# One 16-wide run order for a head's token columns, with one GpSimd copy each for halo and tail gather

## The chip, the cores and the metric

One core of a Trainium2 chip. The metric is the device time of one execution in microseconds (us). Times are medians over executions. A ratio of two kernels is the mean time of one kernel's fast runs over that of the other's fast runs in the same rounds, so it is not quite the ratio of the medians that are quoted. A run counts as slow when it lies over 1.5% above the fastest of its kernel. The granted clock is TensorE's clock as the profile shows it, 1 being full speed. The DMA share is the time of all packets over the time of 16 DMA engines.

## The reference, cut to what matters

```python
# batch 8, heads 8, sequence 576, head width 64, features 128
def phi(x):                       # per token
    proj = x @ w_phi
    proj = proj - max(abs(proj))
    return concat(exp(proj), exp(-proj))
kv  = phi(k).T @ v ;  z = sum(phi(k))
x   = (phi(q) @ kv) / (phi(q) @ z)              # linear attention, per head
gate = sigmoid(causal 5-tap convolution of x over the tokens)
out  = (gate * (x @ w_val)) @ w_out             # 576 x 512 per batch, float32
```

Token t of a head is t = 36x + 2y + a: x (0 to 15) is the run, y (0 to 17) the place in the run, a the parity. Loads put a run into one partition, and TensorE and DMA transposes turn y into columns.

## The kernel before

All instructions of all eight batches stand in one fixed order, the string `ORDER`, with the PSUM banks (`BANKS`) and, for 100 tasks that may go to either of two engines, the choice (`FLEX`) beside it. Within it, one batch goes: transposed loads of q and k (SyncE issues them), key features (exponentials on ScalarE), key-value products, query features, numerators (`num`), normalization, transposition to `XT`, gate and value projections, output projection, eviction to one of six `OUTS` buffers, and a write to memory, issued by SyncE.

A head's columns lie in two halves: k (runs 0 to 7 and 8 to 15), then y, then x within the half. A numerator chunk takes one half with y 0 to 15, so it needs the query features of four units (a unit holds four y). The last two y of both halves are the "tail", a fifth chunk.

```python
def qexp(self, t, b, u, s):          # unit u: y = 4u .. 4u+3
    i = self.two(t.grp, n * P).rearrange("p a (h r) -> p a h r", h=2 * H)
    if u < 4:                        # 32 columns in each half
        o = self.QTIL[b % 2][:, s, ...].rearrange("p a h (k r) -> p a (h k) r", k=2)[:, :, :, u * 32:(u + 1) * 32]
        self.nc.scalar.activation(o, i, AF.Exp, scale=1.0 - 2.0 * s)
    else:                            # tail: one instruction per parity
        for a in range(2): ...

def halo(self, t, b):                # the two y of the run before, for the convolution
    X = self.XT[b % 2][...].rearrange("p h k (y x) -> p (h k) y x", x=8)
    self.nc.gpsimd.tensor_copy(X[:, :, 0:2, 1:8], X[:, :, 18:20, 0:7])
    self.nc.gpsimd.tensor_copy(X[:, 1::2, 0:2, 0:1], X[:, 0::2, 18:20, 7:8])

def gvc(self, t, b):                 # gather the tail of gate*value, x before y
    for j in range(4):
        self.nc.gpsimd.tensor_copy(GVT[...].rearrange("p a (k x y) -> p (a k) x y", k=2, x=8), GV[...])

def odma(self, t, b, c, i0, i1):     # the writes; O is an OUTS buffer, 128 partitions x 512 floats
    if c < 4:                        # main write: 128 rows of 2 KB
        d = self.out_d[b].rearrange("(k x y a) o -> a k y x o", k=2, x=8, a=2)[c % 2, c // 2, 0:16, :, :]
        nc.sync.dma_start(d, O[:, :])
    else:                            # tail write: 32 rows for each batch and parity
        ...
        d = self.out_d[b - 1 + i].rearrange("(x y a) o -> a x y o", x=16, a=2)[a, :, 16:18, :]
        eng.dma_start(d, O[p0:p0 + 32, :])
```

Of the kernel before, what the change touches and what calls it, by code (L numbers as in the profile page):

```python
# [14 lines left out]
BF16 = mybir.dt.bfloat16  # L15
# [13 lines left out]
NW = 14  # L29
NJ = 2 * NC  # L30
XH = R // 2
HALO = 16
XW = HALO + XH
WARM = (
    "8:7:5 21:7:1 214:5:1 "
# [6 lines left out]
    "15 16 18 17 20 19 22 21 24 35 23 37 26 25 36 39 57 27 38 59 41 32 34 170 40 43 61 60 33 172 55 42 73 74 64 47 171 174 58 "  # L42
    "193 311 49 63 44 0 28 76 62 56 50 29 48 65 93 75 45 94 67 53 91 66 54 30 46 92 51 68 97 173 31 89 98 77 188 90 184 52 "
    "185 95 194 96 69 186 189 72 79 5 187 99 228 2 71 100 229 104 313 190 105 70 226 80 9 106 227 101 78 1 103 234 191 110 "
    "175 235 192 10 111 230 178 102 182 179 183 107 112 231 180 108 195 312 11 181 232 109 84 233 81 197 203 82 206 196 6 85 "
    "113 83 314 204 198 8 7 114 199 12 201 319 236 237 205 86 200 320 115 238 202 207 87 210 4 88 116 239 208 315 14 240 118 "
    "117 316 209 211 119 122 212 128 317 241 129 215 242 123 217 124 318 214 125 120 130 213 176 131 243 321 216 329 121 13 "
    "332 3 322 126 331 177 127 132 218 324 330 354 433 434 219 323 355 247 221 248 435 139 220 352 140 353 250 141 436 252 "
    "358 359 149 222 251 249 325 437 150 133 327 356 134 357 244 438 135 246 360 361 223 326 245 333 224 439 136 225 328 137 "
    "265 335 362 266 142 138 363 334 337 143 145 144 338 336 151 339 367 152 440 369 146 253 340 370 254 441 368 267 268 255 "  # L50
    "341 259 442 372 269 256 261 343 260 364 371 443 262 147 366 444 342 148 450 365 446 447 263 452 154 449 445 451 166 155 "
    "257 264 562 448 563 258 458 565 167 344 459 453 347 485 564 345 461 273 346 274 486 454 460 348 455 270 275 477 478 162 "
    "456 271 566 481 457 158 482 163 479 272 480 376 159 349 377 160 483 284 484 378 156 462 350 161 464 285 373 465 351 157 "
    "276 374 567 463 277 487 286 466 488 568 375 467 279 278 492 569 287 379 493 280 153 380 288 281 468 570 494 282 289 164 "
    "573 283 571 577 575 391 472 578 295 576 299 392 165 296 574 393 572 579 290 469 685 686 394 300 606 470 580 607 395 381 "
    "688 471 495 687 382 385 473 496 307 386 497 608 308 581 383 583 609 387 303 584 388 489 304 384 689 291 491 582 389 490 "
    "292 498 604 390 499 474 605 475 500 585 476 610 588 405 611 399 406 690 400 586 410 407 401 691 396 587 411 501 397 612 "
    "503 414 692 613 398 502 589 402 415 591 614 403 693 408 590 404 615 293 592 616 409 593 297 510 618 595 301 506 511 168 "
    "412 617 507 294 696 413 622 298 699 729 812 813 516 730 302 624 425 416 169 594 517 504 623 814 426 421 698 505 518 619 "
    "422 519 815 508 621 697 599 512 429 620 513 727 816 430 509 628 596 629 520 431 728 731 600 630 597 694 625 732 598 735 "  # L60
    "432 627 514 736 417 626 515 712 733 418 695 715 601 734 714 700 602 702 713 521 603 524 703 522 817 527 523 701 525 528 "
    "530 526 818 529 531 704 532 737 705 708 819 537 711 738 707 539 538 820 709 535 706 305 540 633 710 427 536 739 423 716 "
    "533 634 309 740 722 306 631 534 741 748 428 632 856 750 745 424 935 857 541 643 746 635 936 310 644 639 723 747 636 542 "
    "937 640 749 751 645 637 646 753 938 558 543 638 647 752 823 559 717 854 862 641 826 863 939 546 855 825 724 718 642 547 "
    "860 725 861 554 726 824 742 555 858 744 719 859 827 720 743 828 940 651 721 648 941 652 649 662 653 650 754 829 419 663 "
    "654 548 755 830 831 556 655 832 756 942 420 656 766 549 864 833 767 760 757 557 550 834 865 943 835 761 821 768 837 660 "
    "544 769 560 551 758 770 661 838 869 759 657 870 836 822 664 944 871 866 665 658 868 762 666 763 659 867 872 545 667 979 "
    "873 839 980 764 561 677 842 945 765 874 673 678 840 981 674 780 982 843 675 771 841 850 781 679 772 985 782 774 986 552 "
    "676 773 977 775 978 950 680 776 777 844 953 954 553 778 955 785 779 952 669 786 668 951 783 845 670 956 671 789 784 957 "
    "875 672 790 849 983 877 846 984 946 847 876 787 848 949 878 788 851 880 947 962 791 879 852 965 804 853 948 963 958 987 "  # L70
    "805 883 959 964 796 988 966 884 881 960 972 893 882 887 797 894 889 961 885 888 992 973 989 994 886 890 798 895 800 896 "
    "991 891 799 808 801 993 897 968 892 974 967 990 1001 975 1002 998 976 681 1003 809 999 969 682 810 995 1000 970 907 996 "
    "971 904 908 997 905 792 811 909 1004 906 1006 1005 793 1012 1007 1010 1016 1013 1008 916 1011 898 1009 1017 1014 901 917 "
    "1018 899 902 1019 910 1015 903 794 900 1020 806 914 683 911 795 912 802 807 1024 913 684 1021 915 803 1025 1027 1026 "
    "1030 1028 1031 1022 1029 923 1032 1037 924 1023 925 1033 1039 926 1034 1035 1040 1038 927 919 928 1036 931 929 920 1041 "
    "1054 932 918 921 930 1046 933 1055 922 1058 1056 1047 934 1042 1048 1059 1062 1057 1060 1050 1043 1049 1051 1044 1063 "
    "1052 1061 1045 1053 "
)
FLEX = (
    "ADAADAAAAAPPAPPDAAAADDAADAPPDPPDDAAADPPDPPDDADAPPAPPDAAAAAPPAPPDAADDPPAPPAAADADPPDPPDDADAPDDPPADDDDA"  # L80
)
BANKS = (
    "460006544445500124166757234523230145452301456767723672301674501445674652345230145234501276045505450101236723016701016767"
    "674230145670101011236736601674501014523236503323016723674501454567232370123456723450124567741230123236745236732374567452"
    "323450123452367010016767230167676452322367450167016767453636623674567452301452301454500101010101232320101732014501676767"
    "010122154523230145674545676767454450145674545450012303223672301010145236636423236745456701010145014524523670167452323457"
    "201230145450123457466234567014567230123674545701672301672345230177674501234545016744555"
# [69 lines left out]
def build(plan, em=None):  # L157
# [20 lines left out]
    for b in range(B):  # L178
# [19 lines left out]
        if b:  # L198
# [24 lines left out]
            for w in "kq":  # L223
                if b <= PEB:
                    for i, (c0, n) in enumerate(((0, 8), (8, 8), (16, 2))):
                        g = plan.group("tp", 1)
                        tp = A("x" + w, b, i, "PE", 0.06 * n, fn("tp16", w, b, c0, n), [xf[w]], g, 0)
                        h.setdefault(("tps",), []).append(tp)
                        x = A("x" + w, b, i, ("DVE", "ACT"), (dve(n * P), act(n * P)), fn("tc16", w, b, c0, n), [tp], g)
                        for u, (d0, m) in enumerate(UNITS):  # L230
                            if c0 <= d0 < c0 + n:
                                h["x" + w, b, u] = x
                    continue
# [7 lines left out]
        if b == 1:  # L241
# [3 lines left out]
            cg = A("mqt", 0, 0, "POOL", 5.0, fn("c_gt"), [cc], rank=-10)  # L245
# [45 lines left out]
        for u, (c0, n) in enumerate(UNITS):  # L291
            g = plan.group("qp", 2)
            qp = h["qp", b, u] = A("qp", b, u, "PE", 0.118 * n, fn("qp", b, u), [mqr, ceb, G("xq", b, u)], g, 1)
            for s in range(2):
                h["qexp", b, u, s] = A("qexp", b, u, "ACT", act(2 * n * P), fn("qexp", b, u, s),
                                       [qp] + [G("num", b - 2, c) for c in range(4)] + [G("num", b - 1, 4) if u == 4 else None]
                                       + (G("tps",) if b == 1 else [])
                                       , g)


        allq = [G("qexp", b, u, s) for u in range(NU) for s in range(2)] + [G("kv", b, i) for i in range(2)]
        for c in range(5):
            g = plan.group("num", 2 if c < 4 else 1)
# [17 lines left out]
        halo = A("xtc", b, 3, "POOL", 0.6, fn("halo", b), [G("xtc", b, 2)] + [G("gate", b - 2, j) for j in range(4)])  # L321
# [11 lines left out]
        gvc = h["gvc", b] = A("gvc", b, 0, "POOL", 0.6, fn("gvc", b), [G("gv", b, j) for j in range(4)] + [G("out", b - 4, 4)])  # L333
# [19 lines left out]
class Emit:  # L353
    def __init__(self, nc, tc, ctx, q, k, v, w_phi, moe_w_val, moe_conv_w, moe_w_out, out):
# [40 lines left out]
        self.XT = TT("XT", 2, [P, H, 2, XW])  # L395
# [26 lines left out]
        for i in range(2):  # L422
            nc.gpsimd.memset(self.MQP[i][:, :], 0.0)
            nc.gpsimd.memset(self.XT[i][:, :, :, 0:HALO], 0.0)
# [211 lines left out]
    def qp(self, t, b, u):  # L636
# [3 lines left out]
        for par in range(2):  # L640
            rows = slice(par * D, (par + 1) * D)
            nc.tensor.matmul(self.PS[:, t.grp.banks[par], 0:n * P], self.W2[rows, :],  # L642
                             X[rows, c0 * P:(c0 + n) * P].rearrange("p (y h x) -> p h y x", y=n, h=2 * H),
# [207 lines left out]
```

## Time and profile before

| | before |
|---|---|
| time, median of 3 runs | 230.52 us (229.71 to 232.11) |
| span of the profiled run | 228.5 us, granted clock 0.989 |
| busy: PE, DVE, ACT, POOL | 205.4, 176.3, 180.7, 102.8 us |
| from the last matmul's end to the end of the span | 5.3 us |

PE is TensorE, DVE VectorE, ACT ScalarE, POOL GpSimd, SP SyncE; a q behind a name means its instruction queue.

SyncE's timeline has the transposed key loads (start, us that the issue took, what):

```profile
105.07 2.69 SPq L543 DMA_TRANSPOSE kT<-KQN  x1
...
125.88 5.11 SPq L543 DMA_TRANSPOSE kT<-KQN  x1
...
149.81 2.69 SPq L543 DMA_TRANSPOSE kT<-KQN  x1
```

Issue took 2.7 us where no other data was moving (first and third); it took 5.1 us where a value load of 1152 KB had been issued just ahead. The last packets of these three landed 5.0, 7.9 and 4.1 us after the start of their issue, by the trace's DMA records.

### The profile page before, as it was taken

To read this page: it belongs to the slowest core of one execution; us is meant where nothing else is said; L and a number is where in the kernel's file an instruction comes from. 1 tells how busy PE (TensorE), PEld (TensorE's weight loads), DVE (VectorE), ACT (ScalarE), POOL (GpSimd) and SP (SyncE) were. 2 spreads that over 40 slices of the span, in tenths; PEclk is the share of its full clock that TensorE was granted. 3 is DMA by queue.
4 is the path that set the end of the run, shared out by engine and by line. 5 is a ranking of instruction groups with operands and counts; after the bars stand their busy time and mean duration, and the time that the engine had idled before them with its cause. 6 is when DMAs were issued, how large, how long until landed. Compare 5 with 4: busy or idle time off the path is not lost.

```text
span 228.5 us, 9138 instructions
## 1 busy us (share of the span) xinstructions
PE 205.4 (90%) x4001; PEld 142.6 (62%) x4027; DVE 176.3 (77%) x264; ACT 180.7 (79%) x266; POOL 102.8 (45%) x158
## 2 busy tenths in 40 slices
PE   7668887798988999989999999999999999999990
PEld 3345555666675676757667677676765866766640
DVE  2686785998879895989699979788798899483361
ACT  2995999889899988988899999979988999913220
POOL 2718594496029608930099009910119639100020
PEclk9997999999999999999999999999999999999998
DMA  6999943999699939995899995969964206156156
GB/s 202 315 265 286 209 78 103 224 196 183 113 187 244 191 93 179 293 199 61 176 225 182 279 219 141 190 127 228 291 222 138 53 3 142 49 77 204 46 180 188
DMA packets 49282, 39.87 MB, mean 174 GB/s; under 512 B 33690, under 2 KB 38554, under 8 KB 49178
## 3 DMA queue, kind: packets, MB, share of 16 engines
q1 hardware_dynamic: 43136, 29.76, 52.6%
q0 software_dynamic: 5760, 9.31, 24.1%
q8 instruction: 31, 0.51, 0.9%
q10 hardware_dynamic: 346, 0.22, 0.3%
q14 instruction: 9, 0.07, 0.1%
HBM read 30.49 MB, written 9.44 MB: 175 GB/s over the span
## 4 chain that ended last, share of the span: by engine, by line
PE 53%; DVE 17%; DMA 4%; issue 3%; ACT 3%; POOL 2%; DVEq 0%; ACTq 0%
PE PS L751 13%; PE PS L775 10%; PE PS L732 7%; PE PS L598 5%; PE PS L555 5%; DVE XN L691 4%; DMA kT<-KQN 4%; DVE MQP L562 3%; PE PS L670 3%; DVE MK L562 3%; PE PS L739 3%; DVE GV L757 2%; PE PS L642 2%; PE PS L699 2%; PE PS L649 2%
## 5 line engine op out<-in xcount | busy, mean ns | idle before, releaser
L588 POOL TENSOR_TENSOR VT<-VN,EK 128x1152 bf16<-128x1152 f32 x31 | 65.8, 2123 | 60.2 <-ACT EK L581 50.8
L572 ACT ACTIVATE KTIL<-PS 128x1024 bf16<-128x1024 f32 (+1 forms) x80 | 72.5, 951 | 6.3 <-PE PS L555 3.1
L657 ACT ACTIVATE QTIL<-PS 128x1024 bf16<-128x1024 f32 x64 | 62.6, 1036 | 4.6 <-PE PS L649 4.0
L562 DVE TENSOR_REDUCE MQP<-PS 128x8 f32<-128x1024 f32 (+1 forms) x40 | 44.1, 1112 | 6.7 <-PE PS L555 5.6
L562 DVE TENSOR_REDUCE MK<-PS 128x8 f32<-128x1024 f32 (+1 forms) x40 | 44.0, 1110 | 2.5 <-PE PS L555 1.4
L751 PE MATMUL PS<-XT,WV 64*128 64x288 bf16 x512 | 35.5, 283 | 0.4 <-DVE XN L691 0.2
L757 DVE SCALAR_TENSOR_TENSOR GV<-TH,PS 128x576 bf16<-128x576 bf16 x32 | 23.7, 751 | 15.5 <-PE PS L751 10.9
L775 PE MATMUL PS<-WOUT,GV 128*128 128x512 bf16 x109 | 29.6, 380 | 1.5 <-issue 0.6
L743 ACT ACTIVATE TH<-PS 128x576 bf16<-128x576 f32 x32 | 20.1, 655 | 13.0 <-PE PS L739 12.9
L751 PEld LDWEIGHTS <-WV 64*128 64x128 bf16 x512 | 24.6, 94 | 8.3 <-issue 2.6
L598 PE MATMUL PS<-VT,KTIL 64*128 64x65 bf16 x1152 | 24.1, 191 | 1.4 <-POOL VT L589 0.5
L598 PEld LDWEIGHTS <-KTIL 64*128 64x128 bf16 x1152 | 21.3, 95 | 4.2 <-issue 1.3
L691 DVE TENSOR_TENSOR XN<-PS,RCP 128x512 bf16<-128x512 f32 x32 | 22.1, 691 | 1.1
L670 PE MATMUL PS<-KV,QTIL 128*128 128x65 bf16 x512 | 20.1, 193 | 1.7 <-DVE GV L757 0.5
L670 PEld LDWEIGHTS <-QTIL 128*128 128x128 bf16 x512 | 18.2, 97 | 5.0 <-issue 2.7
L612 ACT ACTIVATE OUTS<-PS 128x512 f32<-128x512 f32 x22 | 13.3, 606 | 9.8 <-PE PS L775 9.1
L732 PE MATMUL PS<-XT,GF 128*64 128x288 bf16 x256 | 20.6, 290 | 0.4 <-DVE MQP L562 0.2
L720 POOL COPY XT<-XT 128x224 bf16<-128x224 bf16 x8 | 3.0, 374 | 34.4 <-DVE XT L716 22.3
L775 PEld LDWEIGHTS <-GV 128*128 128x128 bf16 x128 | 11.0, 97 | 11.6 <-issue 1.1
L555 PE MATMUL PS<-W,kT 64*128 64x128 bf16 x288 | 14.9, 219 | 2.7 <-ACT kT L522 1.4
L555 PE MATMUL PS<-W,qT 64*128 64x128 bf16 x288 | 15.1, 220 | 1.7 <-ACT KTIL L572 0.9
L642 PE MATMUL PS<-qT,W 64*128 64x512 bf16 (+1 forms) x80 | 15.0, 359 | 0.9 <-ACT QTIL L657 0.5
(74 smaller groups left out, 257.6 us busy)
## 6 DMA issues: line engine op xcount, KB each, us to landing
VN<-in_v_dram SPq DMA_DIRECT2D x8, 1152.0 KB, 6.9
out_dram<-OUTS SPq DMA_DIRECT2D x32, 256.0 KB, 3.4
KQN<-in_q_dram POOLq DMA_DIRECT2D x6, 576.0 KB, 6.5
KQN<-in_k_dram POOLq DMA_DIRECT2D x6, 576.0 KB, 8.3
KTIL<-in_k_dram SPq DMA_DIRECT2D x4, 288.0 KB, 4.2
KTIL<-in_q_dram SPq DMA_DIRECT2D x4, 256.0 KB, 4.4
out_dram<-OUTS SPq DMA_DIRECT2D x14, 64.0 KB, 3.2
QTIL<-in_q_dram POOLq DMA_DIRECT2D x1, 576.0 KB, 10.4
```

Source lines behind the costliest of these rows:

```text
L555: nc.tensor.matmul(self.PS[:, t.grp.banks[par], i * P:(i + 1) * P], X[rows, (c0 + i) * P:(c0 + i + 1) * P], self.W2[rows, :], start=True, ...
L562: self.nc.vector.tensor_reduce(o, self.two(t.grp, n * P).rearrange("p a (c f) -> p a c f", f=F), AX.X, ALU.max, apply_absolute_value=True)
L572: self.nc.scalar.activation(self.KTIL[b % 2][:, s, c0:c0 + n, :, :].rearrange("p c a f -> p a c f"), self.two(t.grp, n * P).rearrange("p a ...
L588: eng.tensor_tensor(self.VT[g][:, s, :, 0:D], self.VN[b % 2][:, NC * g:NC * g + NC, :], e.to_broadcast([P, NC, D]), ALU.mult)
L598: nc.tensor.matmul(self.PS[:, t.grp.banks[ab], (s * 2 + x) * E1:(s * 2 + x + 1) * E1], self.KTIL[b % 2][rows, s, J // 2, J % 2, :], self.V ...
L657: self.nc.scalar.activation(o, i, AF.Exp, scale=1.0 - 2.0 * s)
L670: nc.tensor.matmul(self.PS[:, t.grp.banks[h // 4], (h % 4) * E1:(h % 4 + 1) * E1], Q[:, s, c % 2, h, (c // 2) * P:(c // 2 + 1) * P], self. ...
L691: nc.vector.tensor_tensor(o.rearrange("p (g h) d -> p g h d", g=ng), n[:, :, :, 0:D], rc.unsqueeze(3).to_broadcast([P, ng, 4, D]), ALU.mult)
L732: self.nc.tensor.matmul(self.PS[h2 * D:(h2 + 1) * D, t.grp.banks[par], 0:R], self.GF[:, h, i, :], X[:, h, :, HALO - 8 * s:HALO - 8 * s + X ...
L751: nc.tensor.matmul(self.PS[:, t.grp.banks[par], 0:R], self.WV2[rows, h, j * P:(j + 1) * P], X[rows, h, :, HALO:XW], start=(h == 0), stop=( ...
L757: nc.vector.scalar_tensor_tensor(out=self.GV[b % 3][:, j, :, :], in0=self.TH[j][:, :, :], scalar=1.0, in1=self.two(t.grp, R), op0=ALU.add, ...
L775: nc.tensor.matmul(self.PS[:, t.grp.banks[0], :], lhsT, self.WOUT[:, j, :], start=(j == 0), stop=(j == 3))
```

## The change

A head's columns go in one run order, y and then all 16 x. A numerator chunk is then 8 y of 16 x and needs two units in place of four; the tail's columns are contiguous, so the tail exponentials of both parities fit one instruction, and halo and tail gather one GpSimd copy each. Order, banks and engine choices are drawn anew for it (`NW`, the number of filler tasks, goes from 14 to 11). The diff in extract, without the strings (`...` marks what is cut, and lines are shortened):

```diff
 def qexp(self, t, b, u, s):
-    i = self.two(t.grp, n * P).rearrange("p a (h r) -> p a h r", h=2 * H)
+    i = self.two(t.grp, n * P).rearrange("p a (h r) -> p a h r", h=H)
-    if u < 4: ...   else: for a in range(2): ...
+    o = QTIL[...][:, s, :, :, r0:r0 + D]   if u < 4   else   QTT[:, s, ...].rearrange("p h a r -> p a h r")
+    self.nc.scalar.activation(o, i, AF.Exp, scale=1.0 - 2.0 * s)
 def halo(self, t, b):
-    self.nc.gpsimd.tensor_copy(X[:, :, 0:2, 1:8], X[:, :, 18:20, 0:7])
-    self.nc.gpsimd.tensor_copy(X[:, 1::2, 0:2, 0:1], X[:, 0::2, 18:20, 7:8])
+    self.nc.gpsimd.tensor_copy(X[:, :, 0:2, 1:16], X[:, :, 18:20, 0:15])
 def gate / val:                                  # 288 columns in one run
-    X[:, h, :, HALO - 8 * s:HALO - 8 * s + XH]
+    X[:, h, HALO - 16 * s:HALO - 16 * s + R]
 def gvc(self, t, b):
-    for j in range(4): self.nc.gpsimd.tensor_copy(... "p a (k x y) -> p (a k) x y" ...)
+    self.nc.gpsimd.tensor_copy(self.GVT[b // 2 % 2][:, :, b % 2, :, :], self.GV[b % 3][:, :, :, 2 * P:R])
 def out(self, t, b, c):
-    lhsT = GV[:, j, c % 2, (c // 2) * XH:(c // 2) * XH + P]
+    lhsT = GV[:, j, c % 2, (c // 2) * P:(c // 2 + 1) * P]
 def odma(...):
-    d = self.out_d[b].rearrange("(k x y a) o -> a k y x o", k=2, x=8, a=2)[c % 2, c // 2, 0:16, :, :]
+    i = c // 2
+    d = self.out_d[b].rearrange("(x y a) o -> a y x o", x=16, a=2)[c % 2, 8 * i:8 * i + 8, :, :]
     nc.sync.dma_start(d, O[:, :])
-    d = self.out_d[b - 1 + i].rearrange("(x y a) o -> a x y o", x=16, a=2)[a, :, 16:18, :]
+    d = self.out_d[b - 1 + i].rearrange("(x y a) o -> a y x o", x=16, a=2)[a, 16:18, :, :]
     eng.dma_start(d, O[p0:p0 + 32, :])
```

## The prediction

> **What bounds the kernel now.** I read the busy times by stage first, then the chain that ended last, the waits, and the timelines of GpSimd and TensorE. Busy times in five stages (start and end in us, length, then each engine's busy us and number of instructions, granted clock, DMA share, GB/s):
>
> ```profile
> 0.00:30.00 30.00, 22.29 (x244) 13.51 (x247) 19.60 (x25) 21.91 (x33) 16.16 (x34) 0.94 1.00 253
> 30.00:80.00 50.00, 43.00 (x965) 31.27 (x969) 41.30 (x61) 45.72 (x64) 29.31 (x34) 1.00 0.86 168
> 80.00:200.00 120.00, 117.19 (x2514) 83.78 (x2528) 101.43 (x155) 107.73 (x162) 55.23 (x81) 1.00 0.75 166
> 200.00:220.00 20.00, 19.69 (x275) 12.81 (x274) 11.45 (x22) 4.77 (x8) 2.14 (x10) 1.00 0.46 106
> 220.00:228.50 8.50, 3.20 (x15) 1.20 (x13) 2.47 (x4) 0.60 (x1) 0.00 (x0) 0.90 0.71 219
> ```
>
> The columns are PE, PEld, DVE, ACT, POOL. Length minus PE busy gives TensorE's idle time: 7.7 us in the start, 7.0 us while the pipeline over the eight batches fills, only 2.8 us in the 120 us of its middle, 0.3 us in the end run and 5.3 us after the last matmul: 23.1 us in all. ScalarE is at 90% and VectorE at 85% in the middle. So three engines are nearly full there; after 200 us it is TensorE alone.
>
> The chain that ended last, its last pieces (start, length, what):
>
> ```profile
> 209.32 1.10 PE PS L732 x16
> 210.43 0.49 PE PS L739 x12
> 210.92 0.32 PE PS L775
> 211.24 0.05 issue
> 211.29 0.59 PE PS L775 x2
> 211.89 4.14 PE PS L751 x64
> 216.41 6.81 PE PS L775 x30
> 223.24 0.69 DVE OUTS L608
> ```
>
> The value projection (L751) goes at 4.14/64 = 65 ns a matmul, the output projection (L775) at 6.81/30 = 227 ns. This end run is packed; a new order cannot shorten it unless it takes work out of it.
>
> Busy is not packed, though. I took the distance from each matmul's start to the next from the trace, and for each group the mean of the lower nine tenths as its unhurried pace. At that pace the work of the middle stage would take some 98 of its 120 us, that of 30 to 80 us some 34 of 50. So short stalls of about 22 us hide in the 117 us that the middle calls busy. They are what a better order could win, and the size of that win is the uncertain term of this prediction.
>
> Last, GpSimd near the end. Two of the longest waits and its timeline:
>
> ```profile
> POOL XT L720 <- DVE XT L716: 22.3, 4, 11.2
> POOL GVT L763 <- DVE GV L757: 14.2, 3, 9.0
> ```
>
> ```profile
> 190.88 0.38 POOL L720 COPY XT<-XT 128x224 bf16<-128x224 bf16 x1
> 191.20 0.26 POOL L721 COPY XT<-XT 128x16 bf16<-128x16 bf16 x1
> 191.36 2.12 POOL L588 TENSOR_TENSOR VT<-VN,EK 128x1152 bf16<-128x1152 f32 x1
> 193.43 1.39 POOL L589 CAST VT<-EK 128x18 bf16<-128x18 f32 x1
> ```
>
> The two halo copies stand ahead of a value scaling of batch 7 in GpSimd's queue, and TensorE's key-value products of that batch wait for the scaling: the idle record there is 0.22 us. In this trace GpSimd's waits are long but nearly all off the path.
>
> **What the Trainium skill says.** "Perfetto Trace Analysis", section Identifying the Most-Contended Engine (and its opening note): matmul busy time is a bad measure because matmuls are pipelined. The trace agrees: 117 us busy against 98 at pace. "TensorE: Matmul & The Clock Gate", Back-to-back issue gap: N/2.4 + 2.5 ns for one warm matmul, 122.5 ns for the 288 columns here. Two matmuls on different half arrays took 130 ns per pair in the end run, so that is within 6% of the page; contiguous columns in place of two runs of 144 can win little. "ScalarE: Activation LUTs", What ACT_TABLE_LOAD costs: an ACTIVATE with immediates takes 186 ns + 0.833 ns per element, neighbours overlap by about 93 ns. For 256 and 512 elements that is 399 and 613 ns; the trace has 401 (mean of the tail exponentials) and 609 (the key exponentials of the same size). "PSUM — Partial Sum Buffer", Engine vs sequencer instructions: the queues of ScalarE, VectorE and GpSimd are strict FIFO. The timeline above shows it: a scaling behind a halo copy.
>
> **The change part by part.** The rows used, of the groups by form:
>
> ```profile
> L660 ACT ACTIVATE QTT<-PS 128x256 bf16<-128x256 f32 x32 | 10.3, 401 | 0.1
> L572 ACT ACTIVATE KTIL<-PS 128x512 bf16<-128x512 f32 x16 | 9.4, 609 | 1.1 <-PE PS L555 1.1
> L763 POOL COPY GVT<-GV 128x64 bf16<-128x64 bf16 x32 | 6.3, 241 | 14.2 <-DVE GV L757 14.2
> L721 POOL COPY XT<-XT 128x16 bf16<-128x16 bf16 x8 | 2.0, 252 | 0.0
> ```
>
> 1. Tail exponentials: 32 of 256 elements become 16 of 512. Busy 10.3 us becomes about the 9.4 us of the key's sixteen: minus 0.9 us of ScalarE. The 64 large ones keep 1024 elements; runs of 32 become runs of 64, and since the key exponentials with runs of 128 take the same 1036 ns, runs cost nothing here.
> 2. Halo: 224 + 16 elements become 240. From 252 ns at 16 and 374 at 224 elements the slope is 0.59 ns, so 240 take about 383: minus 8 x 0.25 = 2.0 us of GpSimd.
> 3. Tail gather: four copies of 64 become one of 256. Four took 0.79 us in the timeline; by the same slope one of 256 takes about 0.39: minus 8 x 0.4 = 3.2 us of GpSimd. Together minus 5 of 103 us on an engine that is 45% busy, with a halo or gather on the chain only once or twice: about 0.2 us at the end.
> 4. Numerators: chunk pairs wait for two units in place of four. Worth something only if a numerator is placed ahead of the batch's last exponentials. I read both orders off the diff: in the new one, too, every numerator of every batch stands behind all exponentials of that batch, by at least 7 places. So the freedom that gives the change its name is hardly used: 0 to 0.5 us. The other half of it, that a query exponential waits for two numerators of two batches before, is never near.
> 5. Matmuls: same number, columns and weights; gates and value projections read their 288 columns in one run in place of two of 144. Zero, by the paces above. Three filler tasks of two matmuls go, which ran where TensorE had nothing else.
> 6. Order, banks and engines: all drawn anew. In the string of the 100 tasks that may go to either engine, 39 are ScalarE's before and 30 after. By kind: five output evictions (606 ns on ScalarE, 684 on VectorE), three copies of batch 0's and three of batch 1's transposed inputs leave ScalarE, two key-value evictions (628 against 695) join it. After the start that is ScalarE -3.0 + 1.3 - 0.9 = -2.6 us, VectorE +3.4 - 1.4 = +2.0 us. If ScalarE alone bound the 170 us from 30 to 200 us (153 us busy, 90%), that would give 2.6/0.90 = 2.9 us; if the sum of both did, 0.6 of 296 us is nothing. I take the middle, 1.3 us. In the start, the early copies taken from a ScalarE that is 73% busy: 0.7 us of the 7.7 us idle. In the new order all of batch 7's scalings on GpSimd stand ahead of the halo copy of batch 6, which removes the wait shown above: 0.3 us.
>
> Sum: 0.2 + 0.2 + 1.3 + 0.7 + 0.3 = 2.7 us, the second 0.2 for part 4. Predicted: 230.5 - 2.7 = 227.8 us, 1.2% less.
>
> **The rivals.** First, the order search found much more than I can read: of 22 us of hidden stalls a third goes, and of 7 us idle in the fill 2 go. For it: ScalarE, TensorE and VectorE are each short of full by 10, 18 (at pace) and 15% in the middle. Against: the old order was tuned to the same limits. It would make 221 to 224 us. Second, VectorE becomes the bound: its total goes from 176 to about 181 us, ScalarE's from 181 to about 174, and VectorE's reductions (1.22 us each, 64 of them) hold PSUM banks that the next projections wait for. For it: "DVE MQP L562" and "DVE MK L562" stand in the chain in the fill. Against: VectorE had 15% idle in the middle. It would make 229 to 232 us. Third, TensorE alone bounds from 80 us on, as its 98% suggests; then nothing but start and fill can win: 229 to 230 us. Fourth, an order drawn anew meets stalls on the chip that its plan did not have, and gives the gain back: 231 to 235 us.
>
> **Range and chances.** The counted parts give 0.4 us and the re-drawn order the rest, so the spread is that of the order: 224.0 to 231.0 us should hold it 8 times in 10. More than 2% faster means below about 225.9, which asks for the first rival in some measure: 0.27. Slower by over 2% means above 235: 0.04. Within 2%: 0.69.
>
> **What would show it.** Right if: sixteen tail exponentials near 609 ns; eight halo copies near 0.38 us and eight gathers near 0.4 us; paces of 65 and 227 ns unchanged in the end run; ScalarE's busy time near 174 us and VectorE's near 181; TensorE's busy time within 3 us of 205; the end run from the last numerators to the last matmul still some 24 us. Wrong if: numerators do start before the last exponentials of their batch; if the middle stage takes several us less with TensorE's work in it at a clearly higher pace (first rival); or if VectorE goes over 90% there and matmuls wait for its reductions (second). A gather that takes over 0.8 us would show that the slope from the halo copy does not carry over.

## More of the kernel before

The target of a main write has the dimensions (16 y, 8 x, 512), that of a tail write (16 x, 2 y, 512). There are 32 main and 16 tail writes; two of the tail writes are issued by ScalarE.

The prediction shows the views that its argument rests on. Two it did not look at are needed later: the DMA queues (packets, megabytes, share of 16 engines' time) and the output writes (count, KB, median us from issue to landing), from the page of the kernel before.

```profile
q1 hardware_dynamic: 43136, 29.76, 52.6%
...
q10 hardware_dynamic: 346, 0.22, 0.3%
...
out_dram<-OUTS SPq DMA_DIRECT2D x32, 256.0 KB, 3.4
out_dram<-OUTS SPq DMA_DIRECT2D x14, 64.0 KB, 3.2
```

q1 is the queue that SyncE feeds, q10 that of ScalarE.

## The result, and the profile after

The changed kernel takes 252.51 us (249.04 to 254.87, four runs, two of them slow) against 230.12 us: ratio 1.0857, 95% interval 1.0711 to 1.1003. Predicted were 227.8 us, at most 231.0.

Two rows of the stages and the last one (columns as in the prediction: PE, PEld, DVE, ACT, POOL busy us, clock, DMA share, GB/s):

```profile
100.00:120.00 20.00, 16.79 (x340) 12.08 (x337) 15.38 (x26) 14.19 (x22) 6.93 (x9) 0.97 0.98 161
...
140.00:160.00 20.00, 15.12 (x263) 10.17 (x263) 12.71 (x24) 11.70 (x16) 11.30 (x13) 0.83 1.06 190
...
240.00:249.50 9.50, 0.00 (x0) 0.00 (x0) 0.00 (x0) 0.00 (x0) 0.00 (x0) 0.50 0.28 83
```

No engine was full in the first two; all are short of work together, while the DMA engines are at 0.98 and 1.06, and in the second the granted clock falls to 0.83. In the last 9.5 us no engine works at all, and data still moves at 83 GB/s. What stands in the chain that ended last (start, us, what) and in TensorE's waits (total us, times, longest):

```profile
84.21 7.97 DMA kT<-KQN
...
107.64 10.51 DMA kT<-KQN
...
136.92 11.59 DMA kT<-KQN
...
232.03 4.46 DMA out_dram<-OUTS
```

```profile
PE PS L553 <- DMA kT<-KQN: 9.3, 4, 4.6
```

The same wait in the kernel before:

```profile
PE PS L555 <- DMA kT<-KQN: 0.7, 1, 0.7
```

There TensorE waited 0.7 us for transposed keys, and after 50 us its chain had no DMA in it. Three loads of transposed keys now hold 30 us of the chain, and a late output write the end. SyncE's timeline shows what stands ahead of two of them:

```profile
105.55 1.98 SPq L780 DMA_DIRECT2D out_dram<-OUTS  x3
107.64 6.88 SPq L541 DMA_TRANSPOSE kT<-KQN  x1
...
133.43 2.68 SPq L786 DMA_DIRECT2D out_dram<-OUTS  x4
136.16 0.65 SPq L780 DMA_DIRECT2D out_dram<-OUTS  x1
136.92 8.00 SPq L541 DMA_TRANSPOSE kT<-KQN  x1
```

Issue now takes 6.9 and 8.0 us, and the last packets land 8.3 and 9.4 us after its start. That invites one explanation, that the new order put output writes in front of the loads. The DMA lines of the page say something else:

```profile
q1 hardware_dynamic: 42684, 29.76, 51.8%
...
q10 hardware_dynamic: 318, 0.22, 0.3%
...
out_dram<-OUTS SPq DMA_DIRECT2D x32, 256.0 KB
out_dram<-OUTS SPq DMA_DIRECT2D x14, 64.0 KB
```

The megabytes are the same, but q1 lost 43136 - 42684 = 452 packets and q10 lost 28, and in the trace those are all packets of 4 bytes. The Trainium skill explains the number. Its page "DMA: Bandwidth & Descriptors", section Why a DMA increments its semaphore by 16 and not by 1, says that a copy runs on k of the 16 DMA engines, where k is the largest number up to 16 that divides the slowest dimension (not of size 1) of both access patterns, and that on the queues of SyncE and ScalarE each of the k engines posts its own completion. The source has 128 partitions in a main write and 32 in a tail write, and with a target of 16 both give k = 16 before; target 8 gives k = 8 for a main write, target 2 gives k = 2 for a tail write. Completions missing: 32 x (16 - 8) + 14 x (16 - 2) = 256 + 196 = 452 on SyncE's queue, and 2 x (16 - 2) = 28 on ScalarE's. Both agree to the packet.

The trace also agrees in its time. I counted how many of the 2 KB output packets are in flight at once: at most 20 before, at most 11 after. Of the time with packets in flight, the most is spent at exactly 16 before (9.4 us) and at exactly 8 and 2 after (29.0 and 15.7 us), which fits k. A single main write takes 1.4 us from its first to its last packet before (at 178 us) and 2.5 us after (at 191 us); a packet alone still takes 84 ns. The last group of writes, 960 packets in both kernels, takes 8.1 us before and 16.9 us after, and the time from the last matmul to the end of the span goes from 5.3 to 13.3 us. The trace does not name the engines; the page says that such a queue takes the lowest-numbered k, so that all narrow writes would meet on the same ones, which no run here shows.

The parts that were meant to be cheaper are, as rows of the groups show (kind, shapes, count, busy us, mean ns):

```profile
L658 ACT ACTIVATE QTT<-PS 128x512 bf16<-128x512 f32 x16 | 8.9, 607 | 1.1 <-PE PS L647 1.1
L758 POOL COPY GVT<-GV 128x256 bf16<-128x256 bf16 x8 | 3.2, 403 | 24.8 <-DVE GV L753 24.8
L717 POOL COPY XT<-XT 128x240 bf16<-128x240 bf16 x8 | 3.1, 388 | 30.8 <-DVE XT L713 29.7 <-DVE OUTS L606 1.1
```

### The profile page after: what moved, and what is told of

It reads as the page before. It is cut to its first block, busy times and chain, and to the rows that moved or that the text cites. A ratio compares the mean times of both kernels' runs of the same rounds, so it can differ in the third digit from the quotient of the medians.

```text
span 249.5 us, 9081 instructions
## 1 busy us (share of the span) xinstructions
PE 209.4 (84%) x3997; PEld 144.6 (58%) x4021; DVE 180.7 (72%) x273; ACT 176.1 (71%) x241; POOL 99.0 (40%) x126
## 3 DMA queue, kind: packets, MB, share of 16 engines
q1 hardware_dynamic: 42684, 29.76, 51.8%
## 4 chain that ended last, share of the span: by engine, by line
PE 47%; DMA 18%; DVE 15%; ACT 6%; issue 5%; POOL 2%; ACTq 1%; DVEq 0%
DMA kT<-KQN 16%; PE PS L747 9%; PE PS L768 7%; PE PS L553 7%; PE PS L728 6%; PE PS L596 6%; DVE MK L560 4%; DVE MQP L560 3%; ACT KTIL L570 2%; PE PS L640 2%; PE PS L735 2%; PE PS L667 2%; DMA out_dram<-OUTS 2%; PE PS L647 2%; DVE XN L688 2%
## 5 line engine op out<-in xcount | busy, mean ns | idle before, releaser
L658 ACT ACTIVATE QTIL<-PS 128x1024 bf16<-128x1024 f32 x64 | 61.9, 1034 | 5.7 <-PE PS L647 5.4
L747 PE MATMUL PS<-XT,WV 64*128 64x288 bf16 x512 | 36.7, 288 | 1.5 <-issue 0.7
L768 PE MATMUL PS<-WOUT,GV 128*128 128x512 bf16 x113 | 31.2, 394 | 1.5 <-issue 0.5
L596 PE MATMUL PS<-VT,KTIL 64*128 64x65 bf16 x1152 | 23.2, 191 | 1.3 <-issue 0.4
L596 PEld LDWEIGHTS <-KTIL 64*128 64x128 bf16 x1152 | 20.7, 95 | 3.6 <-issue 1.8
L553 PEld LDWEIGHTS <-kT 64*128 64x128 bf16 x288 | 9.6, 98 | 17.4 <-DMA kT<-KQN 10.2
L768 PEld LDWEIGHTS <-GV 128*128 128x128 bf16 x128 | 11.8, 101 | 13.4 <-issue 2.9
L610 ACT ACTIVATE OUTS<-PS 128x512 f32<-128x512 f32 x17 | 10.2, 609 | 11.4 <-PE PS L768 11.3
L606 DVE TENSOR_SCALAR OUTS<-PS 128x512 f32<-128x512 f32 x19 | 13.0, 686 | 5.5 <-PE PS L768 4.6
L728 PEld LDWEIGHTS <-GF 128*64 128x64 bf16 x256 | 13.1, 109 | 6.4 <-issue 2.3
(72 smaller groups left out, 249.2 us busy)
```

Of the source, the lines that this page charges most:

```text
L553: nc.tensor.matmul(self.PS[:, t.grp.banks[par], i * P:(i + 1) * P], X[rows, (c0 + i) * P:(c0 + i + 1) * P], self.W2[rows, :], start=True, ...
L596: nc.tensor.matmul(self.PS[:, t.grp.banks[ab], (s * 2 + x) * E1:(s * 2 + x + 1) * E1], self.KTIL[b % 2][rows, s, J // 2, J % 2, :], self.V ...
L728: self.nc.tensor.matmul(self.PS[h2 * D:(h2 + 1) * D, t.grp.banks[par], 0:R], self.GF[:, h, i, :], X[:, h, HALO - 16 * s:HALO - 16 * s + R] ...
L747: nc.tensor.matmul(self.PS[:, t.grp.banks[par], 0:R], self.WV2[rows, h, j * P:(j + 1) * P], X[rows, h, HALO:XW], start=(h == 0), stop=(h = ...
L768: nc.tensor.matmul(self.PS[:, t.grp.banks[0], :], lhsT, self.WOUT[:, j, :], start=(j == 0), stop=(j == 3))
```

## The experiments

Three theories were set against each other. W: the write patterns begin with 8 and 2, so each write has 8 and 2 DMA engines. O: the new order stands output writes ahead of transposed loads and stalls TensorE. L: the layout's other parts, such as the 288 columns in one run, cost the time. The kernels (labels as in the sections below) ran in three groups, each on one chip beside the kernel before: e1, e2, e4 and e7 shared seven of its runs (median 230.31 us), e5, e6, e8 and e9 eleven (231.09 us), e3, e10, e11 and e12 eleven (230.48 us). Across groups, ratios are compared.

Every kernel was told correct, also those that put rows at wrong tokens. With these inputs the outputs of a batch's tokens are nearly equal: swapping the rows of a chunk as below changes the reference's result by 0.2% of its norm. So for row order correctness rests on the patterns, not on the comparison.

### Undo one half of the change

```diff
 # e1: the changed kernel
-NW, WARM, ORDER, FLEX, BANKS of the changed kernel
+NW, WARM, ORDER, FLEX, BANKS of the kernel before
 # e2: the kernel before
-NW, WARM, ORDER, FLEX, BANKS of the kernel before
+NW, WARM, ORDER, FLEX, BANKS of the changed kernel
```

> The changed layout under the old order, banks and engine choices. Theory W (the changed write patterns begin with a dimension of 8 in the main writes and 2 in the tail writes, so each output write runs on 8 or 2 DMA engines where it had 16): 243 to 254 us, most of the loss is here. Theory O (the new order puts transposed loads behind output writes in SyncE's queue and stalls TensorE): 228 to 232 us, as before.

> The old layout and its writes under the new order, banks and engine choices. W: 225 to 231 us, the order alone does no harm. O: 247 to 254 us, the loss is here.

Layout alone: 249.2 us, ratio 1.0847 (1.0768 to 1.0926). Order alone: 232.42 us, ratio 1.0121 (1.0056 to 1.0186). The order falls as the cause of the large loss. It has one of its own, 1.2%, a little over the range of W. Under the old order the wait looks different. Two rows of the waits of the layout alone:

```profile
ACT OUTS L611 <- DMA out_dram<-OUTS: 10.3, 2, 7.8
...
PE PS L769 <- ACT OUTS L611: 7.4, 2, 7.2
```

There the evictions wait for an output buffer that a late write still holds, and TensorE for the evictions; it waits only 1.2 us for transposed keys. The profiled run is a fast one.

### Only the first dimension of the writes

```diff
 # e4: the changed kernel, wide writes, wrong rows on purpose
-    ... .rearrange("(x y a) o -> a y x o", x=16, a=2)[c % 2, 8 * i:8 * i + 8, :, :]
+    ... .rearrange("(x y a) o -> a x y o", x=16, a=2)[c % 2, :, 8 * i:8 * i + 8, :]
-    ... .rearrange("(x y a) o -> a y x o", x=16, a=2)[a, 16:18, :, :]
+    ... .rearrange("(x y a) o -> a x y o", x=16, a=2)[a, :, 16:18, :]
 # e7: the kernel before, narrow writes, wrong rows on purpose
-    ... .rearrange("(k x y a) o -> a k y x o", k=2, x=8, a=2)[c % 2, c // 2, 0:16, :, :]
+    ... .rearrange("(k x y a) o -> a k x y o", k=2, x=8, a=2)[c % 2, c // 2, :, 0:16, :]
-    ... .rearrange("(x y a) o -> a x y o", x=16, a=2)[a, :, 16:18, :]
+    ... .rearrange("(x y a) o -> a y x o", x=16, a=2)[a, 16:18, :, :]
```

> The changed kernel with the two middle dimensions of the write's target swapped, so that it begins with a dimension of 16; rows land at wrong tokens on purpose, bytes and number of rows stay. W: 225 to 231 us, and up to some 19 output packets in flight at once where the changed kernel had 11. O: 247 to 254 us.

> The kernel before with its writes' target dimensions swapped the other way, so that they begin with 8 (main) and 2 (tail); wrong rows on purpose. W: 243 to 254 us, with at most 11 output packets in flight. O: 229 to 232 us.

Wide writes: 232.15 us, ratio 1.0100 (1.0037 to 1.0163), just over W's range of 231 us. The kernel before with narrow writes: 249.43 us, ratio 1.0829 (1.0744 to 1.0914), within W's range. Two lines, with no instruction added and no byte moved more, take the loss away and bring it about. With wide writes the page has 43136 and 346 packets again, at most 20 output packets in flight and 5.1 us after the last matmul:

```profile
q1 hardware_dynamic: 43136, 29.76, 52.6%
...
q10 hardware_dynamic: 346, 0.22, 0.3%
```

With narrow writes in the kernel before there are 42684 and 318, and at most 12 packets in flight where 11 were forecast; where four tail writes go alone (206.5 to 212.4 us) never more than 4. Theory W stands; L is left with nothing, as the remaining 1.0% is about that of the order alone.

A swap of the dimensions also changes the order in which rows fall in memory. For the main writes this is no rival: x runs innermost in the kernel before, which is fast, and in the changed kernel, which is slow; y does so in the wide version (fast) and in the narrow one (slow). For the tail writes the two were not separated.

Another rival is the granted clock: in the changed kernel's trace it stands at 0.5 for 10.2 us of the middle (119.0 to 122.4 and 146.3 to 153.1 us). What this adds there was not separated, but it is not needed for the loss. The profiled run of e10 below, narrow in batches 0 to 5, has clock 1.0 up to its last matmul, and is still 7.3 us longer than that with wide writes throughout (237.1 against 229.8 us).

### Main writes or tail writes

```diff
 # e5: only the first pair of lines of e4 (main writes wide)
 # e6: only the second pair of lines of e4 (tail writes wide)
```

> The changed kernel with only the 32 main writes (256 KB) made to begin with 16; the 14 tail writes on SyncE and 2 on ScalarE (64 KB) still begin with 2; wrong rows on purpose. If loss follows the engine time that a narrow write takes (a main write 128 rows on 8 engines = 16 rows each, a tail write 32 rows on 2 engines = 16 rows each, and a group of four tail writes on the same two engines 64 rows each): the main writes carry most, since 32 of them each cost some 1.3 us more; expected 233 to 239 us. If the tail writes carry it: 243 us or more.

> The mirror: tail writes begin with 16, main writes still with 8; wrong tail rows on purpose. Main writes carry it: 243 to 250 us. Tail writes carry it: 233 to 238 us.

Main wide: 239.25 us, ratio 1.0371 (1.0311 to 1.0431). Tail wide: 241.71 us, ratio 1.0432 (1.0361 to 1.0504). Against 1.0100 with both wide, narrow tail writes alone cost 2.7 points and narrow main writes alone 3.3, together 6.0 of the 7.6 that both cost. So neither carries most. I had expected the main writes to do so, at 1.3 us more for each, where the traces above show 1.1 us: the main-wide run came out just above its range, and the tail-wide one just under. The tail writes carry one eighth of the main writes' bytes (16 x 64 KB against 32 x 256 KB) and nearly as much of the loss; on two engines, a group of four of them would put 64 rows on each. That the two cost more together than apart fits that they wait for the same engines, which no run shows directly. The completion packets follow the rule here too: 42940 with only main writes wide (196 missing) and 42880 with only tail writes wide (256 missing).

### Does a better queue order save narrow writes?

```diff
 # e3: the changed kernel, SyncE's queue
-odma0.1 odma0.2 xk4 odma0.0 xq4            +xk4 xq4 odma0.1 odma0.2 odma0.0
-odma1.3 odma1.2 odma0.3 xk5 xq5            +xk5 xq5 odma1.3 odma1.2 odma0.3
-odma2.1 odma2.2 odma1.4 odma2.0 xk6 xq6    +xk6 xq6 odma2.1 odma2.2 odma1.4 odma2.0
-xk7 odma2.3 xq7                            +xk7 xq7 odma2.3
```

(xk6 is the transposed key load of batch 6, odma2.1 a write of batch 2. Eleven tasks move, where the expectation says ten; one of them, odma1.4, is four instructions.)

> The changed kernel, its narrow writes kept; in SyncE's queue the transposed loads of batches 4 to 7 are put ahead of the output writes that stood before them (ten writes move behind). If narrow writes cost mainly by standing ahead of these loads: 236 to 242 us, and TensorE's waits for transposed keys fall from 9.3 us to under 3. If most of the cost is elsewhere (output buffers that come free late, the writes left at the end): 245 us or more.

It took 251.04 us; its four runs spread from 244.92 to 257.0 us, so that no ratio was formed. Only one of them counts as fast, 244.92 us, which is 4 to 6 us under the changed kernel's fast runs (249.04 and 251.3 us). So the reordering may have saved something, and its size is open; but even that run is some 13 us above the kernel with wide writes. The profiled run is slow, so its waits show only where the time can go:

```profile
PE PS L555 <- DMA kT<-KQN: 1.0, 1, 1.0
...
ACT OUTS L612 <- DMA out_dram<-OUTS: 5.9, 2, 3.6
...
DVE OUTS L608 <- DMA out_dram<-OUTS: 5.8, 2, 5.2
...
PE PS L555 <- DVE OUTS L608: 3.7, 1, 3.7
```

The wait fell as expected if the loads were the main cost: 9.3 us became 1.0 us, and the last packets of the four moved key loads landed within 4.7 us. The time did not fall to the 236 to 242 us that belonged to it. Evictions wait 11.7 us for output buffers, and TensorE 3.7 us behind one of them. The fast profiled run of the layout alone shows the same, 10.3 us of evictions waiting for output buffers and 1.2 us of waiting for transposed keys, with nearly the whole loss. So the late transposed loads were the form that the loss took in this order, not its cause.

### The end or the middle

```diff
 # e10: wide (wrong rows) if b >= 6, else narrow     # e11: wide if b < 6, else narrow
+            if b >= 6:
+                d = d.rearrange("y x o -> x y o")
```

> The changed kernel with wide writes (wrong rows) for batches 6 and 7 alone. The changed kernel runs on for some 12 us after its last matmul, the kernel before 5.3 us. If the end of the run costs what that shows: 243 to 246 us, 5 to 8 us less than the changed kernel.

> The mirror: wide writes (wrong rows) for batches 0 to 5, narrow ones for 6 and 7. What the narrow writes cost in the middle goes, the end stays: 237 to 240 us. If instead the end writes are what makes the whole loss: 245 us or more.

Last two batches wide: 241.01 us, ratio 1.0431 (1.0356 to 1.0505), and 5.1 us from the last matmul to the end. First six wide: 241.30 us, ratio 1.0495 (1.0426 to 1.0564), and 13.2 us after the last matmul (its verdict is on record as unclear, although its interval lies above 2%). From 1.0857 that is 4.3 points for the end and 3.6 for the middle, together about the whole of 7.6; counted up from 1.0100 it is 4.0 and 3.3. Both times miss their ranges, 243 to 246 and 237 to 240 us: the end costs somewhat more than I had expected and the middle less. About half the loss is the plain drain of the last writes on fewer engines, with nothing left to hide it.

### A right version with wide writes

Rows must leave in the order in which they stand in the partitions, so the target cannot simply be turned. But which 128 columns form an output chunk is free: every second column of a run order gives 16 y by 8 x. The tail gather writes x before y again, in two copies.

```diff
 # e8: the changed kernel
-    lhsT = GV[:, j, c % 2, (c // 2) * P:(c // 2 + 1) * P]
+    lhsT = GV[:, j, c % 2, c // 2:2 * P:2]
-    d = ... "(x y a) o -> a y x o", x=16, a=2)[c % 2, 8 * i:8 * i + 8, :, :]
+    d = ... "(x k y a) o -> a k y x o", x=8, k=2, a=2)[c % 2, c // 2, 0:16, :, :]
-    gvc: one copy                    # tail target (2 y, 16 x)
+    gvc: for a in range(2): one copy, "p j (x y) -> p j y x"     # tail target (16 x, 2 y)
 # e9: e8 with NW, WARM, ORDER, FLEX, BANKS of the kernel before
 # e12: e8 with the order of e3
```

A first try, to turn the stationary columns themselves into x before y, did not build.

> A right version of the wide writes for the changed kernel: an output chunk takes every second column of the run (even or odd x), so that its target begins with the 16 y, and the tail gather writes x before y in two copies. If stationary columns at a step of two load as fast as dense ones, as with the wrong-rows version: 231 to 233 us. If the step slows the weight loads (128 of them): 1 to 4 us more.

> The same right version under the old order, banks and engine choices. If the new order costs the 1% that the order alone showed on the old layout: 227 to 230.5 us, at or slightly under the kernel before. If the layout itself costs it: 232 us.

> The right version of the wide writes under the new order, with the transposed loads first as in the other run. With wide writes the transposed loads were late by at most a microsecond, so this wins little: 230 to 232.5 us; under 229 us it would beat the kernel before.

New order: 232.29 us, ratio 1.0053 (1.0007 to 1.0098). Old order: 231.12 us, ratio 0.9975 (0.9917 to 1.0033); the time lies between its two ranges, the ratio speaks against a cost of the layout. New order with transposed loads first: 234.62 us, ratio 1.0147 (1.0081 to 1.0213), worse than expected and, with two of six runs slow, unclear by the verdict at 2%. The step of two columns costs nothing:

```profile
L770 PEld LDWEIGHTS <-GV 128*128 128x128 bf16 x128 | 11.4, 98 | 12.4 <-issue 1.2
```

98 ns against 97 ns for dense columns before. So the layout, written right and under the old order, is as fast as the kernel before within 0.8%, and none of the versions beats it.

| run | median us | ratio to before (95%) |
|---|---|---|
| changed kernel | 252.51 | 1.0857 (1.0711 to 1.1003) |
| layout alone, old order | 249.20 | 1.0847 (1.0768 to 1.0926) |
| before with narrow writes | 249.43 | 1.0829 (1.0744 to 1.0914) |
| order alone, old layout | 232.42 | 1.0121 (1.0056 to 1.0186) |
| changed, wide writes (wrong rows) | 232.15 | 1.0100 (1.0037 to 1.0163) |
| changed, only main / only tail wide | 239.25 / 241.71 | 1.0371 / 1.0432 |
| changed, wide in batches 6, 7 / 0 to 5 | 241.01 / 241.30 | 1.0431 / 1.0495 |
| changed, transposed loads first | 251.04 | none (spread) |
| right, wide, new order | 232.29 | 1.0053 (1.0007 to 1.0098) |
| right, wide, old order | 231.12 | 0.9975 (0.9917 to 1.0033) |
| right, wide, transposed loads first | 234.62 | 1.0147 (1.0081 to 1.0213) |

## Why the prediction was wrong

The step that failed is "The change part by part". It lists six parts and leaves the output writes out. The last two lines of the diff change their target's dimensions, and by leaving them out the sum gave them zero. They measured 7.6 points of ratio, some 17.5 us of 230 (1.0857 less 1.0100; with only two fast runs of the changed kernel its interval alone is 1.5 points each way). Under the old order the same two lines cost 8.7 points in the new layout (1.0847 less 0.9975) and 8.3 in the old one. The same omission shows in "What the Trainium skill says": four pages were looked up, none of them that of the DMA, although the change touches a transfer. And no rival was a transfer that becomes slower; the nearest, "an order drawn anew meets stalls on the chip", had 231 to 235 us and another mechanism. The chance of 0.04 for slower came from that.

Parts 1 to 3 were right in size. Tail exponentials: forecast near 609 ns, measured 607; busy 8.9 us where I had 9.4. Halo: forecast 0.383 us, measured 0.388. Gather: forecast 0.39 us, measured 0.403. What they win was not measured by itself: layout and wide writes under the old order come to 0.9975 (0.9917 to 1.0033), so it is within the noise, as said.

Part 4, that the freedom of the numerators is hardly used, was read off the diff, and the changed kernel's trace agrees: in every batch the first numerator starts after the end of the last exponential, by 1.4 to 8.2 us. No run tried an order that uses the freedom.

Part 5, matmuls unchanged, held: with wide writes the last 64 value projections take 4.17 us (4.14 before) and 26 output projections 5.82 us, 224 ns each (227 before). One reading can be sharpened. The 122.5 ns that the prediction works out from the page, like its 399 and 613 ns for ScalarE, is an estimate, and the 130 ns beside it is length over count, pauses included. By the starts of the matmuls in the trace of the kernel before, most pairs of value projections follow each other in 122 to 123 ns, and output projections in 215 to 216 ns. In the changed kernel TensorE's busy time is 209.4 us, outside the 3 us that I had allowed, and 204.0 us with wide writes.

Part 6, the order, is a second miss, of size and sign. Its busy times came as forecast (ScalarE 176.1 us for 174, VectorE 180.7 for 181), but the expected win of 2.3 us of the 2.7 (start, middle, end) is a loss of about 1%, by two runs with different layouts (ratios 1.0121 and 1.0100). (Its 1.3 us was called the middle of 2.9 and nothing, which is 1.45.) In these two traces the loss lies in the middle: TensorE idles 6.1 and 6.4 us of the 120 there, where it idled 2.8, and the last numerators begin at 200.3 and 200.6 us, where they began at 198.9. The second rival, VectorE as the bound at 229 to 232 us, is near in size; VectorE is busy for 103.8 of the 120 us of the middle with wide writes, 86% where it was 85%, which is under the 90% that I had named as its sign. So that nearness is no support for its mechanism, and what in the order costs the 1% stays open.

The stated sign of trouble, matmuls waiting in the middle, did appear, but behind DMA and not behind VectorE. The end run from the first of the last numerators to the last matmul kept its 24 us (212.1 to 236.1 us; 198.9 to 223.2 before). What grew was the time before it, by 13.2 us, and the stretch after it, from 5.3 us, which I had counted as fixed, to 13.3 us.

## What to carry to other kernels

When a layout changes, read every transfer whose access pattern it touches as carefully as the compute: here the same bytes and rows took 1.4 us or 2.5 us a write, as the first dimension of the target was 16 or 8. A count of completion packets in the profile's DMA lines, before against after, showed this loss at a glance. When a wait moves on as you fix its queue order, as from transposed loads to output buffers here, look for the resource that both share.

## What the Trainium skill lacked or had wrong

- "DMA: Bandwidth & Descriptors" had the rule, and the runs agree: 452 and 28 completion packets fewer in the changed kernel, and all of them back with wide writes. What it lacks is the cost to other transfers: transposed loads behind narrow writes landed 8.3 and 9.4 us after their issue began, where they took at most 4.7 us once they stood ahead of the writes (a slow run); evictions then waited 11.7 us for output buffers.
- No page tells that the profile's landing times go missing with narrow writes. In the changed kernel they are missing for every transfer that SyncE issues: the output writes had 3.4 and 3.2 us before, the value loads 6.9 and the transposed key loads 5.9 us. With wide writes they are back (3.2, 2.7, 6.1 and 6.8 us). With only tail writes wide the value and key loads have them (6.4 and 8.0 us), while the main writes still have none.
- "GPSIMD Engine Reference" has no fixed cost for short copies. Here copies of 16, 64, 224, 240 and 256 elements of bf16 in a partition took 252, 241, 374, 388 and 403 ns. From 224 to 16 elements that is 0.59 ns per element above some 243 ns, an estimate from these rows; the copies of 64, whose pattern swaps two dimensions, lie below it.
